# K and Q turned in one transfer, k turned in its own order, later loads on the Pool queue, a shorter mask product and a plan tuned anew, in a kernel of a long convolution and a memory attention

## Chip, cores and metric

One core of one Trainium2 chip. The time is device microseconds of one execution. A profile is one execution with the hardware profiler on; its span is from the first to the last instruction, some 2 us shorter than the time of the same execution. "Granted clock" is the share of its full rate that TensorE was granted, averaged over the span.

## The reference, cut to what matters

Two independent parts stand side by side; their outputs are concatenated. All data are bf16.

```python
# part A: S = 2048 positions, 640 channels
k_shift = sum(k_pad[:, t:t + S] * shift_k[:, 3 - t] for t in range(4))   # 4 taps
kv = k_shift * v
y = causal_convolution(kv, ssm_k) + kv * ssm_D       # by Fourier transforms in the reference
a = q * y

# part B: x is 2048 x 640, 32 heads of 20, N = 4 segments of L = 512
for s in range(4):
    logits = qs @ ks.T * scale + mask                # causal inside a segment
    o = g * (phi(qs) @ M) / (phi(qs) @ z) + (1 - g) * softmax(logits) @ vs
    M, z = M + phi(ks).T @ vs, z + phi(ks).sum()
b = concat_heads(o) @ wo
```

## The kernel before

Python records every operation with a key, prices it, and a list scheduler (`plan`) fixes one order for each engine from priorities; `BIAS` and `HOLD` are tables of tuned corrections to them. So an edit of a table or a price can move any instruction. The queue of an engine is in order, its DMA issues included.

Part B runs in 8 units (4 segments times 2 halves of the heads). A unit projects x to K, Q and V, turns K and Q (so that the head dimension lies on the partitions), bounds the logits from the largest |K|, and makes scores, exponential and products.

```python
def wload(engs, half):            # weights; w0: first half of the heads, w1: second half
    def f():
        for i, (w, eng) in enumerate(zip((B_wk, B_wq, B_wv), engs)):
            eng.dma_start(out=self.wqkv[:, :, half, i, :], in_=...)
# "w0", "w1", "wo", "Wf", "Wi" and xT all load from nc.sync (SP)

def proj(tci):                    # four token blocks a unit; KQ has two buffers
    KQ = self.KQ[:, tci % 2]
    for i in range(3):
        ...                       # five products of xT and wqkv
        nc.scalar.copy(out=dst, in_=...)                 # the cast to KQ or Va
    nc.sync.dma_start_transpose(out=self.KTs[u][:, :, tok], in_=KQ[:, 0, :, :])
    nc.sync.dma_start_transpose(out=QT[:, :, tok], in_=KQ[:, 1, :, :])

def bound():
    V.tensor_reduce(out=kam[:], in_=self.KTs[u][:], axis=AX.X, op=ALU.max, ...)   # needs only K
    ...                           # A = sel * kam; PqT = phi(QT)
    V.tensor_scalar(out=qabs..., in0=QT..., ...)         # |Q|, needs Q
    for g in range(4):
        nc.tensor.matmul(pb[0:16, :], lhsT=A[:, g, :], rhs=qabs[:, g, :], ...)    # "tq,A" in the profile

def attn(g):
    ...
    if masked:
        for hl in range(4):
            nc.tensor.matmul(st[:, hl, 0:384], lhsT=self.ident[:], rhs=self.nmask[:], start=True, stop=False)
    for (kc, c0) in spec:         # scores on top of it, four row strips at once
        ...
# [cut: part A loads v and q in four pieces each from nc.sync, and turns k in four strided transfers to kr]
```

The softmax here doesn't subtract the row's maximum and nothing guards it: scores larger than these inputs give would overflow.

## Time and profile before

| | before |
|---|---|
| time, median of 3 | 328.97 us (328.57 to 334.71) |
| span of the profile | 331.0 us, granted clock 0.975 |
| TensorE / VectorE / ScalarE busy | 287.2 / 272.7 / 266.0 us |
| first product | 12.56 us |

The prediction shows the lines of the page and of the timeline. In a timeline line the columns are start, duration, engine and source line, operation, output and inputs, shapes, count, and in brackets the engine's idle time before it and what ended that. All operations carry the line of one helper, so tiles are told apart by name.

One thing the prediction did not read belongs here too. Before the change the work of the bound falls in two steps, the largest of K (`kam`) while Q's turn is still on its way:

```profile
25.18 2.29 DVE L441 TENSOR_REDUCE kam<-KT 128x4 f32<-128x2048 bf16 x1 [0.82 <-DMA KT<-KQ]
27.50 0.23 DVE L441 TENSOR_TENSOR A<-sel,kam 128x64 bf16<-128x64 bf16 x1
29.60 0.69 DVE L441 TENSOR_SCALAR tq<-QT 128x2048 int16<-128x2048 int16 x1 [1.87 <-DMA QT<-KQ]
```

(VectorE's timeline, kernel before, first unit.) VectorE waits for K 0.82 us and for Q 1.87 us; the 2.29 us in between cost nothing. TensorE, in the same unit, waits for the last of these three:

```profile
30.35 1.35 PE L441 MATMUL ab<-tq,A 128*16 128x512 bf16 x4 [1.52 <-DVE tq L441]
```

### The profile page before, as it was taken

The numbers are of one execution on the slowest core, as the hardware profiler recorded it, in microseconds if no ns is written. First come the engines' busy times: TensorE is split into PE (matmuls) and PEld (weight loads), VectorE is DVE, ScalarE is ACT, GpSimd is POOL, SyncE is SP. The second block draws the span as 40 slices with busy tenths as digits, with TensorE's granted clock in tenths as the row PEclk, the third lists the DMA queues.
The fourth block names the chain that finished last, engine by engine and source line by source line (L and its number), as shares of the span: only waits on it lengthen the run. The fifth ranks groups of instructions, "written<-read, shape, count | busy, mean of one in ns | idle before, by whom it ended". The sixth has DMA issues, their size and how long they took to land. (4 is left out here: it accounts for less than half of the span.)

```text
span 331.0 us, 8829 instructions
## 1 busy us (share of the span) xinstructions
PE 287.2 (87%) x3673; PEld 199.6 (60%) x3674; DVE 272.7 (82%) x455; ACT 266.0 (80%) x351; POOL 30.4 (9%) x58
## 2 busy tenths in 40 slices
PE   0498899989999995999999995999989997897982
PEld 0375766666767674566857662676765664564641
DVE  0016859999998979999997597799999999999942
ACT  1176699799998998899898887878899999668711
POOL 5001100000000010000101010300010001330310
PEclk9998999999999999799999998999999999998998
DMA  8945954646405986813321669504303452324272
GB/s 251 224 95 125 253 95 94 124 125 111 81 2 141 201 136 155 209 50 81 70 59 53 119 135 188 139 6 77 66 20 69 60 79 60 98 49 126 66 138 79
DMA packets 97159, 35.65 MB, mean 108 GB/s; under 512 B 90000, under 2 KB 95168, under 8 KB 96864
## 3 DMA queue, kind: packets, MB, share of 16 engines
q1 hardware_dynamic: 94816, 30.01, 43.7%
q0 software_dynamic: 1872, 4.76, 5.5%
q8 instruction: 28, 0.46, 0.6%
q10 hardware_dynamic: 432, 0.34, 0.3%
q14 instruction: 11, 0.09, 0.1%
HBM read 13.46 MB, written 5.24 MB: 56 GB/s over the span
## 5 line engine op out<-in xcount | busy, mean ns | idle before, releaser
L441 ACT ACTIVATE ET<-st 128x1536 bf16<-128x1536 f32 (+1 forms) x96 | 154.9, 1614 | 23.1 <-PE st L441 22.4
L441 PE MATMUL ab<-wqkv,xT 128*128 128x320 bf16 x480 | 75.9, 304 | 13.3 <-DMA wqkv<-in_B_wk_dram 12.6
L441 PEld LDWEIGHTS <-xT 128*128 128x128 bf16 x480 | 45.1, 99 | 33.3 <-DMA xT<-in_B_x_dram 10.6
L441 PEld LDWEIGHTS <-ET 128*128 128x128 bf16 x1280 | 42.3, 96 | 10.2 <-issue 6.6
L441 ACT CAST F<-ab 128x512 bf16<-128x512 f32 x80 | 45.4, 615 | 2.3 <-PE ab L441 1.6
L441 PE MATMUL o<-Va,ET 128*128 128x21 bf16 x1280 | 44.1, 173 | 2.3 <-DVE o L441 1.9
L441 PE MATMUL st<-QT,KT 32*128 32x128 bf16 (+3 forms) x512 | 34.8, 303 | 8.7 <-ACT ET L441 8.5
L441 ACT CAST KQ<-ab 128x320 bf16<-128x320 f32 x64 | 28.0, 461 | 14.9 <-PE ab L441 14.4
L441 DVE TENSOR_TENSOR S<-S 128x2048 bf16<-128x2048 bf16 (+1 forms) x40 | 37.0, 941 | 0.0
L441 PEld LDWEIGHTS <-Wf 128*128 128x128 bf16 x320 | 28.1, 97 | 11.8 <-issue 7.9
L441 PE MATMUL st<-nmask,ident 128*128 128x384 bf16 x128 | 26.4, 329 | 2.8 <-ACT ET L441 2.7
L441 PEld LDWEIGHTS <-KT 32*128 32x128 bf16 x512 | 11.8, 91 | 28.2 <-issue 26.3
L441 PE MATMUL ab<-wo,oT 128*128 128x320 bf16 (+1 forms) x140 | 22.4, 300 | 4.1 <-ACT outb L441 3.5
L441 PE MATMUL ab<-kT,Wf 128*128 128x256 bf16 x160 | 23.6, 273 | 0.9 <-ACT F L441 0.2
L441 POOL DMA_DIRECT2D out_dram<-outa x20 | 15.3, 767 | 93.0 <-DVE outa L441 85.3
L441 DVE TENSOR_TENSOR o<-o,rr 128x320 bf16<-128x320 f32 x48 | 23.2, 484 | 0.5
L441 PE MATMUL ab<-vt,Wf 128*128 128x256 bf16 x160 | 22.0, 273 | 1.3 <-DVE vt L441 1.2
L441 DVE TENSOR_TENSOR ET<-ET,cmask 128x1024 bf16<-128x1024 bf16 x32 | 21.6, 675 | 1.6 <-ACT ET L441 1.6
L441 DVE TENSOR_TENSOR S<-Xh,Kh 128x4096 bf16<-128x4096 bf16 x10 | 22.8, 2278 | 0.0
L441 PEld LDWEIGHTS <-oT 128*128 128x128 bf16 x160 | 14.1, 100 | 13.7 <-issue 6.5
L441 PE MATMUL ab<-skd,kr 128*128 128x128 bf16 x320 | 22.0, 227 | 0.3 <-DVE vt L441 0.2
L441 DVE RECIPROCAL rr<-o 128x16 f32<-128x16 f32 (+1 forms) x64 | 15.3, 239 | 7.3 <-PE o L441 7.3
(70 smaller groups left out, 402.7 us busy)
## 6 DMA issues: line engine op xcount, KB each, us to landing
sk<-in_A_ssm_k_dram SPq DMA_DIRECT2D x5, 512.0 KB, 3.9
vt<-in_A_v_dram SPq DMA_DIRECT2D x20, 128.0 KB, 3.2
qd<-in_A_q_dram SPq DMA_DIRECT2D x20, 128.0 KB, 3.3
out_dram<-outa POOLq DMA_DIRECT2D x20, 128.0 KB, 2.6
out_dram<-outb POOLq DMA_DIRECT2D x12, 160.0 KB, 2.6
Wf<-c_wf SPq DMA_DIRECT2D x1, 1024.0 KB
Wi<-c_wi SPq DMA_DIRECT2D x1, 1024.0 KB
wqkv<-in_B_wq_dram SPq DMA_DIRECT2D x2, 400.0 KB, 5.5
```

Of the source, the lines that this page charges most:

```text
L441: f(*[fix(a) for a in args], **{k: fix(v) for k, v in kw.items()})
```

## The change

The intent: fewer issues on the SP queue, which is late with its turns, and less TensorE time.

```diff
-    nc.tensor.matmul(st[:, hl, 0:384], lhsT=self.ident[:], rhs=self.nmask[:], ...)
-    for (kc, c0) in spec:
+    nc.tensor.matmul(st[:, hl, 0:256], lhsT=self.ident[:], rhs=self.nmask[:], ...)
+    parts = ... if not masked else [(3, 0, 0, 128), (2, 128, 0, 128), (2, 128, 128, 256)]
+    for (kc, c0, a, b) in parts:          # the last part has no mask under it and starts its own sum

-    nc.sync.dma_start_transpose(out=self.KTs[u][:, :, tok], in_=KQ[:, 0, :, :])
-    nc.sync.dma_start_transpose(out=QT[:, :, tok], in_=KQ[:, 1, :, :])
+    nc.sync.dma_start_transpose(out=self.KQT[half][:, :, :, tok]..., in_=KQ...)

-    kr = ring("kr", [128, 4, KPAD + 512]); for c in range(4): dma_start_transpose(kr[:, c, ...], k rows c::4)
+    kr = ring("kr", [128, KPAD + S]);      for n in range(2): dma_start_transpose(kr[:, 1024 n ...], k rows in order)
-    lhsT=kr[:, cc, p0:p0 + 128]
+    lhsT=kr[:, first:first + 509:4]

-    "Wi": nc.sync ...   "w1": (nc.sync,) * 3   "wo": nc.sync ...   vt, qd: nc.sync
+    "Wi": nc.gpsimd ... "w1": (nc.gpsimd,) * 3 "wo": nc.gpsimd ... vt (but the first), qd: nc.gpsimd
# [cut: prices of two kinds of operation, how BIAS and HOLD enter plan, finer keys, and both tables anew]
```

The last cut is no detail: with it every engine gets another order. On SP the first loads, `Wf, sk, x, wq, wk, ident, wv` before, become `wk, wq, Wf, x, wv, sk`.

## The prediction

> **What bounds the kernel now.** I read the page first (busy shares, slices), then the waits, then the timeline of single stretches where TensorE stood still, and then single tiles.
>
> ```profile
> PE 287.2 (87%) x3673; PEld 199.6 (60%) x3674; DVE 272.7 (82%) x455; ACT 266.0 (80%) x351; POOL 30.4 (9%) x58
> ...
> PE   0498899989999995999999995999989997897982
> ```
>
> TensorE is the fullest engine, and in the second line (40 slices of 8.3 us, tenths) it stands at 9 or more nearly everywhere between the first two slices and the last two; slices 16 and 25 are the deep dips. VectorE and ScalarE follow at 80%, so there is no single owner: TensorE bounds the middle when nothing blocks it, and a chain of matmul, exponential, matmul (one PSUM area "st" for all scores) takes over where it is blocked. I split TensorE's 331.0 - 287.2 = 43.8 us of idle time: 12.6 us before the first product, about 7.5 us after 318.2 us (the drain: 12.8 us with some 5 us of products in it), so about 23.7 us in the middle. The middle is thus 93% full. Its largest holes, from the timeline of TensorE and of ScalarE:
>
> ```profile
> 12.56 2.83 PE L441 MATMUL ab<-wqkv,xT 128*128 128x320 bf16 x10 [12.56 <-DMA wqkv<-in_B_wk_dram]
> ...
> 128.40 1.91 ACT L441 ACTIVATE PqT<-QT 128x2048 bf16<-128x2048 bf16 x1 [1.05 <-DMA QT<-KQ]
> ...
> 131.70 0.40 PE L441 MATMUL st<-QT,KT 32*128 32x512 bf16 x4 [2.52 <-ACT ET L441]
> ```
>
> ```profile
> 201.03 1.91 ACT L441 ACTIVATE PqT<-QT 128x2048 bf16<-128x2048 bf16 x1 [2.89 <-DMA QT<-KQ]
> ...
> 203.31 0.84 PE L441 MATMUL ab<-wo,oT 128*128 128x320 bf16 x5 [3.23 <-ACT outb L441]
> ```
>
> Both dips have one story: ScalarE, in order, stands before the exponential of the turned Q, which waits for its transfer; then that 1.91 us exponential goes ahead of the work that would free PSUM, and TensorE stops for 2.52 and 3.23 us. Why the transfer is late shows in the timeline of the SP queue just before the second:
>
> ```profile
> 190.16 1.90 SPq L441 DMA_DIRECT2D qd<-in_A_q_dram  x3
> 192.16 1.25 SPq L441 DMA_TRANSPOSE QT<-KQ  x1
> 193.45 0.59 SPq L441 DMA_DIRECT2D qd<-in_A_q_dram  x1
> 194.14 2.13 SPq L441 DMA_TRANSPOSE KT<-KQ  x1
> 196.38 1.20 SPq L441 DMA_TRANSPOSE QT<-KQ  x1
> 197.68 4.24 SPq L441 DMA_TRANSPOSE oT<-o_s  x3
> ```
>
> The queue issues without a break: a load of q for a later stage (2.5 us in four pieces) stands between the turns of K and Q, and the last turn of Q begins to be issued only at 196.38.
>
> **What the Trainium skill says.** (1) "Perfetto Trace Analysis", section "What 'DMA-bound' means", says that a queue solid with issue slices shows descriptor generation rather than data movement; the section "DMA Optimizations" advises spreading issues over the engines that can issue. The SP queue above agrees. (2) "DMA: Bandwidth & Descriptors", "SWDGE vs HWDGE vs iDMA": issues from Pool have their descriptors written by software on Pool's cores, and a plain DMA transpose must come from SP or ACT; so only the plain loads can move, as done. (3) "SBUF — State Buffer", "SBUF: two separate sides": VectorE operations in a two-port mode lock Pool out while it writes descriptors. In this trace Pool's 20 stores of 512 pieces took 750 to 907 ns with VectorE 82% busy, so I see no starvation. (4) The same page, "Door 1: The DMA port swizzle", says that a stride is free while consecutive accesses share a 16-byte line, for bf16 up to 8 elements. The trace has such a case, below, and agrees.
>
> **The change part by part.**
>
> *Mask product.* The timeline of one masked block:
>
> ```profile
> 40.88 0.81 PE L441 MATMUL st<-nmask,ident 128*128 128x384 bf16 x4 [0.54 <-ACT ET L441]
> 41.62 0.34 PE L441 MATMUL st<-QT,KT 32*128 32x128 bf16 x8
> ```
>
> One such matmul takes 326 ns (median), four overlap into 0.81 us, so they follow at (0.81 - 0.326) / 3 = 161 ns, which is 384 columns at 2.4 per ns (estimate from these rows). At 256 columns that is 107 ns: 4 x 54 = 0.216 us less for each of 32 blocks, 6.9 us. Against it the 256-wide score product of each head is cut into two 128-wide ones, 128 more matmuls and weight loads (3674 to 3802). Short matmuls follow at about 25 ns (28 of "o" in 0.85 us), so 4 x 25 = 0.1 us a block as the most, 3.2 us; about half if the shorter streams overlap as four row strips do. Net: 3.7 to 5.3 us of TensorE time, taken as 4.5. It lies in the middle, which is 93% full, and also in the chain through "st": I count 4 of it.
>
> *K and Q in one transfer, k in its own order.* 64 issues of 1.22 us become 32 of double size, 20 issues of k at 1.26 us become 10. The issue of xT, five times the size, took 2.78 to 3.35 us, so one more 128 KB costs 0.4 to 0.5 us; a double one some 1.7 us (estimate). SP time: 78 + 25 = 103 us become 54 + 17 = 71 us. The bytes stay. K's turn now waits for Q's cast too (about 0.5 to 1 us later for the bound), while Q lands about 0.6 us sooner.
>
> *Weights of k with a stride of 4 elements.* The load of sk has this stride today: its weight loads take 113 ns in the median, those of kr 98. But the rate counts:
>
> ```profile
> 36.02 1.07 PE L441 MATMUL ab<-skd,kr 128*128 128x128 bf16 x16
> 36.92 0.61 PE L441 MATMUL ab<-ident,sk 128*128 128x128 bf16 x8
> ```
>
> A single one lasts 219 ns in both, so the spacing is (1.07 - 0.22) / 15 = 57 ns without and (0.61 - 0.22) / 7 = 56 ns with the stride. I count zero; the weight-load rows alone will grow by 320 x 15 ns = 4.8 us, hidden.
>
> *Plain loads to Pool.* 16 vt, 20 qd, three weights, Wi and wo leave SP: 36 x 0.6 + about 2.5 = 24 us of SP queue. With the turns SP is relieved of some 56 us, a sixth of the span. Pool's busy time rises from 30.4 to about 60 us (36 x 0.76 + 5 x 0.6), which costs nothing by itself. What the two queue parts gain are the stalls behind late turns: 2.52 + 3.23 us, and 0.76 + 0.51 + 1.04 us at the neighbouring waits of the same pattern (also at 240 us), 8 us in all. Half is kept back, since the exponential of the turned Q still occupies ScalarE: 4 us.
>
> *Start and drain.* The new order brings wk and wq ahead of Wf and xT, and sk behind. The first product needs wk and xT: 0.4 + 0.4 + 1.0 + 0.64 MB stand at or ahead of xT, where 2.95 MB stood ahead of its last need before. But 0.4 to 1.2 MB of weights of the second half now start on Pool at once and share the 16 DMA engines. I take 1 us. At the end eight products of part A move behind the first twelve of the last projection, where TensorE waited for the last turn: 0.5 us.
>
> *New priorities.* All orders change. The rest of the middle's holes, some 16 us, may grow or shrink; I take zero, with 4 us to each side.
>
> Sum: 4 + 4 + 1 + 0.5 = 9.5 us off 329.0, so **319.5 us**.
>
> **The rivals.** (a) *The chain through "st" holds:* each head group makes three rounds of scores and exponential (1.90 and twice 1.47 us of ScalarE, 155 us in all), and with ScalarE at 80% and VectorE at 82% the freed TensorE time turns into waiting for "ET". For it: 12.4 us of TensorE's waits are on ET today. Against: nearly all of those holes are short, and the long ones come from the late turn. It would give 324 to 327. (b) *Pool's queue becomes the in-order trap that SP was:* loads of v and q now stand behind stores that wait for their results (85 us of such waits by Pool). If they come late, the products of v stall. Against: v and q are issued a stage ahead, and landing took 2.6 us from Pool and 3.2 us from SP. It would give 325 to 332. (c) *The new order is better than its parts:* with 282 us of TensorE work, a middle filled to 95% rather than 93% ends near 11.5 + 279 / 0.955 + 12.8 = 316; with less waiting at the start, 313.
>
> **Range and chances.** My number is the sum of the parts; (c) sets the low end, 313.5, (a) the high end, 326. Faster by 2% means under 322.4, inside the range and 3 us above my number, so faster 0.67, same 0.31. Slower would need (b) in full: 0.02.
>
> **What would show it right or wrong.** Right: TensorE busy near 282 to 283 us; the mask product at about 272 ns a piece and 0.54 us for four; spacing of the k products still 57 ns while their weight loads take 113 ns; 42 turns fewer on SP, SP's breaks back; no wait over 1 us of ScalarE for the turned Q; the holes of 2.5 and 3.2 us gone. Wrong in the mask step: the twelve short score products last over 0.45 us. Wrong in the queue step: VectorE or TensorE wait for vt or qd, or TensorE's idle time in the middle stays near 24 us with other releasers. Wrong in the start: a first product later than 12.6 us, because the Pool loads take the DMA engines.

## The result and the profile after

The changed kernel takes 345.5 us (median of 4, 344.28 to 348.43), against 330.39 us (median of 4) of the kernel before: ratio 1.049, interval 1.038 to 1.060, so slower by 5%, where 3% faster was predicted. All four of its runs are fast; of the four of the kernel before, one (334.71 us) counts as slow and is left out of the ratio. The granted clock of the two profiles is the same (0.976 and 0.975). A ratio here is the mean time of one kernel's fast runs over the mean of the other's fast runs of the same rounds, so not quite the ratio of the quoted medians. Runs over 1.5% above the fastest of their kernel count as slow. The kernel before scatters by some 3% (328 to 338 us), so the mean of its fast runs depends on its fastest run; where a verdict is fine I give the medians too (they are over all runs, slow ones included).

The page after:

```profile
PE 283.5 (83%) x3801; PEld 199.4 (58%) x3802; DVE 272.6 (80%) x455; ACT 265.4 (78%) x351; POOL 61.6 (18%) x99
...
PE   0058799799898799998779979999979998788892
```

TensorE is busy 3.7 us less, Pool twice as long, both much as predicted. The slices (8.5 us each here) show where time went: two empty ones lead, not one, and the third is half full (before it stood at 9).

```profile
20.89 8.31 PE L442 MATMUL ab<-wqkv,xT 128*128 128x320 bf16 x45 [20.89 <-DMA xT<-in_B_x_dram]
```

(TensorE's timeline, after.) The first product starts at 20.89 us instead of 12.56, and waits for x's turn instead of wk. From first product to end it is 321.0 us, before 318.4: so 8.3 of the 10.9 us of longer span lie ahead of the first product, and the other 2.6 us, where 4 us and more of gain were expected, lie behind. The start on SP and on Pool (timelines, after):

```profile
0.74 0.46 SPq L442 DMA_DIRECT2D wqkv<-in_B_wk_dram  x1
1.25 0.51 SPq L442 DMA_DIRECT2D wqkv<-in_B_wq_dram  x1
1.81 0.52 SPq L442 DMA_DIRECT2D Wf<-c_wf  x1
2.38 8.46 SPq L442 DMA_TRANSPOSE xT<-in_B_x_dram  x1
```

```profile
3.89 0.86 POOL L442 DMA_DIRECT2D wqkv<-in_B_wv_dram  x1
...
7.40 0.88 POOL L442 DMA_DIRECT2D wqkv<-in_B_wk_dram  x1
```

1.8 MB (wk, wq, Wf) are issued ahead of x's turn, and while it is under way (from 2.38 us to its landing at 20.89) Pool starts two 0.4 MB loads of second-half weights (and at 12.87 us a third), which nothing needs yet. Before, x's turn was issued at 1.64 us, behind Wf and sk.

```profile
8.00:18.00 10.00, 0.00 (x0) 0.00 (x0) 0.00 (x0) 0.00 (x0) 1.15 (x2) 1.00 1.25 135
```

(Stretches, after; the last two columns are the DMA share and GB/s.) From 8 to 18 us the DMA engines are full, with packets overlapping (1.25), but move only 135 GB/s. Before, from 8 to 14 us, they moved 279 GB/s:

```profile
8.00:14.00 6.00, 1.44 (x6) 0.94 (x7) 0.00 (x0) 0.00 (x0) 0.00 (x0) 1.00 1.15 279
```

Why the rate is so low isn't settled: b_w1_pool below, with the same loads from Pool beside x's turn, moved 290 GB/s in the same stretch.

The second place is a pause at 113 us. Timelines after of ScalarE, TensorE, SP and Pool, in this order:

```profile
112.97 0.42 ACT L442 CAST KQ<-ab 128x320 bf16<-128x320 f32 x1 [3.53 <-DMA KQT<-KQ]
```

```profile
113.45 1.19 PE L442 MATMUL ab<-wqkv,xT 128*128 128x320 bf16 x5 [3.55 <-ACT KQ L442]
```

```profile
105.36 4.90 SPq L442 DMA_TRANSPOSE KQT<-KQ  x2
```

```profile
101.47 2.96 POOL L442 DMA_DIRECT2D vt<-in_A_v_dram  x4 [22.29 <-PE ab L442]
104.42 0.55 POOL L442 DMA_DIRECT2D Wi<-c_wi  x1
```

The cast may not write its buffer of KQ until the joint turn has read it; that turn, issued at 105.36 us, lands 7.5 us later (3.4 us in the median), with the 1 MB of Wi and four pieces of v in flight. The two pauses that the prediction aimed at are gone from their places, but this one stands in, and another of their kind appears where no turn is late:

```profile
256.67 0.34 PE L442 MATMUL st<-KQT 32*128 32x384 bf16 x4 [2.66 <-ACT ET L442]
```

Ahead of it ScalarE starts the exponential of the turned Q at 252.89 us without any wait; its 1.96 us stand before the exponential that TensorE needs.

The prediction's details held: mask products of 273 ns, four in 0.60 us (0.54 was predicted, but its own figures, 0.81 less 0.216, make 0.59); the twelve short scores 0.34 us; sixteen products of kr in 1.06 us, so still 56 to 57 ns apart.

```profile
49.39 0.60 PE L442 MATMUL st<-nmask,ident 128*128 128x256 bf16 x4 [0.16 <-ACT ET L442]
49.92 0.34 PE L442 MATMUL st<-KQT 32*128 32x128 bf16 x12
```

### The profile page after: what moved, and what is told of

Same layout as the page of the kernel before. It is cut to its first block, busy times and chain, and to the rows that moved or that the text cites. A ratio compares the mean times of both kernels' runs of the same rounds, so it can differ in the third digit from the quotient of the medians.

```text
span 341.9 us, 8967 instructions
## 1 busy us (share of the span) xinstructions
PE 283.5 (83%) x3801; PEld 199.4 (58%) x3802; DVE 272.6 (80%) x455; ACT 265.4 (78%) x351; POOL 61.6 (18%) x99
## 4 chain that ended last, share of the span: by engine, by line
PE 36%; ACT 20%; DVE 19%; DMA 12%; issue 9%; POOL 1%; SPq 1%; ACTq 0%; DVEq 0%; POOLq 0%
PE ab L442 25%; ACT ET L442 10%; PE st L442 6%; DMA xT<-in_B_x_dram 5%; PE o L442 5%; DMA KQT<-KQ 5%; DVE Xh L442 4%; DVE S L442 4%; ACT F L442 4%; ACT KQ L442 2%; DVE ET L442 2%; DMA out_dram<-outb 2%; DVE o L442 1%; DVE kam L442 1%; ACT kT L442 1%
## 5 line engine op out<-in xcount | busy, mean ns | idle before, releaser
L442 PE MATMUL ab<-wqkv,xT 128*128 128x320 bf16 x480 | 77.5, 309 | 25.4 <-DMA xT<-in_B_x_dram 20.9
L442 PEld LDWEIGHTS <-xT 128*128 128x128 bf16 x480 | 45.3, 100 | 47.2 <-DMA xT<-in_B_x_dram 20.9
L442 ACT CAST KQ<-ab 128x320 bf16<-128x320 f32 x64 | 26.5, 436 | 32.9 <-PE ab L442 28.5
L442 PEld LDWEIGHTS <-ET 128*128 128x128 bf16 x1280 | 41.6, 96 | 17.5 <-issue 12.6
L442 ACT CAST F<-ab 128x512 bf16<-128x512 f32 x80 | 44.4, 627 | 2.4 <-PE ab L442 2.0
L442 PE MATMUL st<-KQT 32*128 32x128 bf16 (+2 forms) x640 | 35.0, 275 | 6.1 <-ACT ET L442 5.7
L442 DVE TENSOR_SCALAR xm<-KQ 128x640 bf16<-128x640 bf16 x12 | 3.8, 318 | 30.6 <-ACT KQ L442 30.6
L442 PEld LDWEIGHTS <-KQT 32*128 32x128 bf16 x640 | 13.3, 92 | 23.6 <-issue 21.4
L442 PE MATMUL ab<-kT,Wf 128*128 128x256 bf16 x160 | 22.6, 273 | 2.5 <-ACT kT L442 1.1
L442 PE MATMUL st<-nmask,ident 128*128 128x256 bf16 x128 | 19.3, 273 | 4.4 <-ACT ET L442 3.8
L442 POOL DMA_DIRECT2D vt<-in_A_v_dram x16 | 11.9, 752 | 54.4 <-PE ab L442 34.7
```

What stands on the lines that cost most here:

```text
L442: f(*[fix(a) for a in args], **{k: fix(v) for k, v in kw.items()})
```

## The experiments

**Theories.** S (start): x's turn shares the DMA engines with weights loaded ahead of it and beside it from Pool, and the late first product moves the whole kernel. J (joint landing): one transfer of K and Q takes from the bound the step in which K was worked on while Q travelled. N: the new order is the worse one, rather than (P) bulk loads on Pool in the middle that delay turns. M: the loss lies in the middle, not at the start. Rivals in each case: the time would stay when the part is undone.

Fourteen kernels ran (a gap in the table: the profile fell on a slow execution). In each, the engines' order was kept and only the named operations were changed after planning. All gave right results. The kernel before had medians of 333.1, 333.1, 332.8, 332.8 and 332.9 us in the five sessions, of which the first three ran on one chip and the other two on two others. The medians in the table are over all runs (a_split's and b_rest's take in one of 862 and one of 629 us), the ratios over the fast ones.

| run | base | what differs | median us | ratio (95%) | first product us | clock |
|---|---|---|---|---|---|---|
| after | | the change | 345.5 | 1.049 (1.038–1.060) | 20.89 | 0.976 |
| a_w1_sp | after | w1 on SP, behind sk | 337.3 | 1.015 (1.012–1.019) | 14.01 | 0.973 |
| a_split | a_w1_sp | K and Q turned singly | 336.1 | 1.018 (1.011–1.025) | | |
| a_order | a_split | and v, q, Wi, wo on SP | 335.7 | 1.013 (1.007–1.018) | 13.40 | 0.979 |
| a_xfirst | after | x first on SP | 334.1 | 1.011 (1.007–1.015) | 7.53 | 0.970 |
| a_both | a_xfirst | and w1 on SP | 334.9 | 1.015 (1.010–1.021) | 7.57 | 0.970 |
| a_xsplit | a_xfirst | K and Q turned singly | 332.9 | 1.003 (1.000–1.005) | 7.71 | 0.981 |
| b_w1_pool | before | w1 early on Pool | 335.7 | 1.008 (1.004–1.012) | 16.72 | 0.985 |
| b_mask | before | mask product only | 329.3 | 0.990 (0.986–0.994) | 12.37 | 0.982 |
| b_turns | before | joint turn, k in own order | 349.7 | 1.052 (1.048–1.056) | 12.39 | 0.970 |
| b_kq | before | joint turn only | 350.0 | 1.059 (1.049–1.068) | 12.41 | 0.957 |
| b_kr | before | k in own order only | 332.0 | 1.005 (1.001–1.008) | 12.41 | 0.992 |
| b_pool | before | v and q on Pool only | 333.2 | 1.006 (1.002–1.010) | 12.34 | 0.977 |
| b_rest | before | mask, k, v and q | 331.6 | 0.996 (0.993–0.999) | 12.58 | 0.977 |
| b_start | b_mask | x first on SP | 327.2 | 0.985 (0.978–0.992) | 7.93 | 0.990 |

### The start

**a_w1_sp.**

```diff
+ w1 = [o for o in order if o.key[:2] == ("load", "w1")]    # second-half weights
+ each of w1: issued by sync instead of gpsimd, right behind sk
```

> The changed kernel with its orders kept on every engine, except that the three weight loads of the second half (wqkv, 400 KB each) are issued from SP right behind sk instead of from Pool at once. Theory S (sharing): in the changed kernel these loads, started on Pool at 3.9 and 7.4 us, take turns with the first turn of x on the 16 DMA engines and make it land at 20.9 us. Then the first product comes at 12 to 14 us here and the whole is 7 to 9 us shorter than the changed kernel (345.5 down to about 337.5, still 2% above the kernel before). Rival O (order on SP): wk, wq and Wf ahead of xT are what makes it late; then the first product stays near 20 us and the time does not move by more than 2 us.

8.2 us faster than the changed kernel (medians), first product at 14.01 us.

```profile
14.01 8.63 PE L442 MATMUL ab<-wqkv,xT 128*128 128x320 bf16 x45 [14.01 <-DMA xT<-in_B_x_dram]
```

So loads that nothing needed, only started early from another queue, held x's turn back by 6.9 us, and the end followed: by 8.2 us in the medians, of two sessions, by 4.5 us in the spans of the two profiles (341.9 to 337.4). The rest to 12.56 us, 1.5 us, I put down to the order on SP itself (wk and wq ahead of x's turn). The Trainium skill, "DMA: Bandwidth & Descriptors", section "Issuing engines are not separate DMA queues", says that transfers of all issuing engines run on the same 16 DMA engines and interleave. This run agrees, and puts a price on it.

**b_w1_pool**, the same loads moved the other way in the kernel before:

```diff
+ each of w1: issued by gpsimd instead of sync, near the start of Pool's queue
```

> The kernel before with its orders kept, except that the same three loads go to Pool, right after its first constant, at about 3.9 us. The reverse test. S: xT lands late and the first product moves from 12.6 us to 17 to 21 us, the time grows by 4 to 8 us (to 333 to 338). O: the first product stays within 1.5 us of 12.6 and the time within 2 us.

The first product moved by 4.2 us, 12.56 to 16.72, so sharing holds in this order too: x's turn landed 11.8 us after its issue instead of 8.9. Both figures fall a little short of theory S's (17 us and 4 us): the median moved only by 2.6 us. A late start is not always paid one to one.

**a_xfirst**, only the order of six loads of the changed kernel:

```diff
- sync: wk, wq, Wf, x, wv, sk
+ sync: x, wk, wq, wv, Wf, sk
```

> The changed kernel with only the first six loads on SP in another order: x first, then wk, wq, wv, Wf, sk (it had wk, wq, Wf, x, wv, sk). The three second-half weights stay early on Pool. Theory S (the loss is at the start, because x's turn shares the DMA engines and comes last): x's turn is then issued before Pool's first bulk load starts at 3.9 us; first product at 8 to 12 us instead of 20.9, and the time falls by 7 to 12 us: ratio 1.013 to 1.028. Theory M (the new order loses it in the middle): the first product comes earlier, but the end moves by less than 4 us: ratio over 1.037.

```profile
0.74 2.79 SPq L442 DMA_TRANSPOSE xT<-in_B_x_dram  x1
```

```profile
7.53 1.49 PE L442 MATMUL ab<-wqkv,xT 128*128 128x320 bf16 x5 [7.53 <-DMA wqkv<-in_B_wk_dram]
```

(SP and TensorE of a_xfirst.) The early Pool loads are all still there. Ahead of them, x's turn is issued in 2.79 us instead of 8.46, and the first product comes at 7.53 us. The time falls by 11.4 us (9.6 by the spans), within the 7 to 12 us expected. Theory S holds, and by the medians no other single edit of the changed kernel gains as much; but the first product is now 5 us ahead of the kernel before, so this is more than the start had lost.

**a_both** moves the second-half weights back as well.

> The same order of first loads, and the second-half weights also on SP behind sk. The version with those weights on SP alone had 1.0153 with its first product at 14.0 us. Theory S: first product at 8 to 9 us, and the end follows by 4 to 6 us: ratio 0.997 to 1.004. Theory M: 1.010 or more.

A miss. The first product is as early as in a_xfirst, and the span equal (332.4 and 332.3 us), so once x is first, the Pool loads at the start cost nothing visible. The expected 0.997 to 1.004 did not come: the ratio is 1.015, which is theory M's, by medians 1.006 (334.88 over 332.79). The session had a fast run of the kernel before (328.27 us), which lowers the mean of its fast runs. By ratio the end did not follow the earlier first product at all (a_w1_sp has the same 1.015), by span it followed by 5.0 us (337.4 to 332.4), by medians by 2.4; which of these is right the runs don't settle. What is safe is that a first product 5 us ahead of that of the kernel before doesn't make this kernel faster than it: something else costs.

### The joint turn

**b_turns** puts the joint turn and k's own order into the kernel before:

```diff
- sync.dma_start_transpose(K half); sync.dma_start_transpose(Q half)
+ sync.dma_start_transpose(K and Q)        # where the later of the two stood
- four strided turns of k; + two in its own order
```

> The kernel before, same order of every engine, with K and Q turned in one transfer (at the place of the later of the two) and k turned in two transfers in its own order and read with a stride. My prediction's step: about 3 to 4 us less, because the waits of ScalarE for the turned Q (1.05, 2.89, 0.92 us) shrink. Rival W: the merged transfer lands later than the first of the two did and keeps both halves of KQ from being rewritten until then; then casts into KQ wait, the gain is under 1 us or it is slower. The strided weights should cost nothing: spacing of the k products 57 ns with weight loads of 113 ns.

16.6 us slower than before (medians): as much as the whole change. Rival W has the direction right and its sign is there (casts into KQ wait 4.0 us for the joint turn), but 4.0 us is not 16.6. **b_kq** and **b_kr** part the two:

```diff
b_kq:  + the joint turn of K and Q alone
b_kr:  + k in its own order alone
```

> The kernel before, same order of every engine, with only K and Q turned in one transfer (k as before, in four). Theory J (joint landing): what cost 17 us in the run with both turns merged is that the reduction of K (2.29 us on VectorE, eight times) now waits until Q has landed too, while it used to run during Q's turn. Then this run is again about 15 to 17 us slower than before (near 348), VectorE waits for the merged transfer before the reduction by 12 us or more in sum. Rival R (k's order or its strided weights): this run is within 3 us of the kernel before.

> The kernel before, same order, with only k turned in its own order, two transfers in place of four, read with a stride of 4. J: within 1.5 us of the kernel before, spacing of the k products unchanged at 57 ns. R: slower by 10 us or more.

b_kr is neutral, so the stride of the weights of k is free, as counted, and halving its issues gains nothing. b_kq alone is 16.9 us slower. Waits of VectorE for `kam`, before and in b_kq (columns: us in all, times, longest):

```profile
DVE kam L441 <- DMA KT<-KQ: 1.0, 2, 0.8
```

```profile
DVE kam L441 <- DMA KQT<-KQ: 17.8, 8, 6.3
```

In all eight units VectorE, in order, now stands before the reduction. First unit of b_kq, VectorE and TensorE:

```profile
31.68 2.29 DVE L441 TENSOR_REDUCE kam<-KQT 128x4 f32<-128x2048 bf16 x1 [6.27 <-DMA KQT<-KQ]
34.00 0.23 DVE L441 TENSOR_TENSOR A<-sel,kam 128x64 bf16<-128x64 bf16 x1
34.14 0.68 DVE L441 TENSOR_SCALAR tq<-KQT 128x2048 int16<-128x2048 int16 x1
```

```profile
34.88 1.87 PE L441 MATMUL ab<-tq,A 128*16 128x512 bf16 x4 [5.00 <-DVE tq L441]
```

The reduction starts at 31.68 instead of 25.18 us: the last half to land now releases both. The 2.29 us of K's work, once beside Q's turn, lies on the path, and TensorE's pause grows from 1.52 to 5.00 us. Of the 4.5 us by which TensorE's product comes later (34.88 against 30.35), K's work is thus 2.3; the other 2.2 go with the later landing of Q's half. Nor did the queue get its time back: three joint turns in a row take

```profile
20.14 7.72 SPq L441 DMA_TRANSPOSE KQT<-KQ  x3
```

2.57 us each, while a free joint turn is issued in 1.27 us, a single one in 1.22. Theory J's time and waits came in the old order; how much of the 16.9 us is K's lost step and how much the later landing, no run separates. One caution: keeping the old order is harsh on the joint turn, since the reduction stays placed for an early K.

**a_split** turns K and Q singly in the changed kernel's order (on top of a_w1_sp):

```diff
- sync.dma_start_transpose(K and Q)
+ sync.dma_start_transpose(K half); sync.dma_start_transpose(Q half)
```

> The changed kernel with the weights of the second half on SP (as in the run a_w1_sp) and, new, K and Q turned in two transfers again, K first, at the place of the merged one; all else and all orders kept. J: the new order already sets the reduction of K late (it waits 1.2 us in all), so the joint landing costs little here: 0 to 3 us less than a_w1_sp. If the merged transfer still holds the chain here, 4 us or more less.

No difference from a_w1_sp beyond the intervals: in the changed kernel's order VectorE waits only 1.2 us in all for the joint turn ahead of the reduction, against 17.8 us in b_kq, so the new order had placed it late already. One execution of this kernel, the profiled one, took 862 us, and its profile isn't used. **a_xsplit** repeats the split on top of a_xfirst:

> The version with x first, with K and Q turned in two transfers, K first. If the joint turn makes the 3.45 us pause at 103 us: the pause waiting for KQ goes (K's half of the buffer is free earlier), with it one of the five half-clock stretches (1.71 us each), together 3 to 5 us: ratio 0.996 to 1.003. If the bulk load of Wi on Pool makes it (it shares the DMA engines with either form of turn): the pause stays over 2 us and the ratio is 1.007 to 1.014.

1.0025 against 1.0111: a gain of 0.9% by the ratios, 0.4% by the medians (334.1 to 332.9), while the pause stays:

```profile
101.29 0.84 PE L442 MATMUL ab<-wqkv,xT 128*128 128x320 bf16 x5 [2.81 <-ACT KQ L442]
```

So each expectation got one half right: the time is the first one's, the pause (2.81 us after 3.45) the second one's. Wi was issued 0.6 us ahead of the turns in this run too. In a_order, with Wi on SP behind the turns, this pause is gone; TensorE waits 1.30 us for Wi itself instead. I take the pause as made mainly by the bulk load beside the turn, and the joint turn as costing 0 to 3 us in the new order (a_split shows no gain, a_xsplit 1 to 3 us).

### The remaining parts

**b_mask:**

```diff
- matmul(st[:, hl, 0:384], ident, nmask);  + matmul(st[:, hl, 0:256], ident, nmask[:, 0:256]) and three score parts
```

> The kernel before, same order of every engine, with the mask product 256 wide and the third score product cut in two (the mask constant stays 384 wide in memory). My prediction's step: 4 us less (about 325 against 329), one mask product 272 ns, TensorE busy near 282.7 us. Rival (chain through st holds): TensorE's busy time falls the same, the time by 0 to 1.5 us only, and idle time before score products grows by what was saved.

3.9 us faster by medians, 3.3 by the ratio of 0.990. This is the part of the change that pays.

**b_pool:**

```diff
- v (from the second chunk on) and q: sync;  + gpsimd
```

> The kernel before, same order, with the 16 later loads of v and the 20 loads of q issued from Pool. My prediction's step: the stalls behind late turns of Q shrink (2.89 and 1.05 us of ScalarE), 2 to 4 us less. Rival (in-order trap or sharing): loads wait behind stores, or turns land later because Pool's loads take turns with them; then 0 to 4 us more.

No gain; 1.006 is on the rival's side. Some 22 us less on SP's queue (36 issues of 0.6 us) did nothing for the time, although in this profile the stalls that the prediction counted on did shrink: ScalarE waits 1.2 us for the turned Q, once, instead of 4.9 us. Such waits vary between profiles (3.8 us in b_mask, 4.7 us in b_rest, which has the same loads on Pool), but nothing of them came through to the time here: those stalls were not worth what they measured.

**b_rest**, mask product, k's own order and Pool loads together in the old order:

> The kernel before, old order, with the shorter mask product, k in its own order and vt and qd on Pool: all parts of the change that were neutral or good alone. If the parts add, 0.990 x 1.0045 x 1.006 = 1.001, so 0.996 to 1.006; if k's shorter queue time and the Pool loads help only once SP and TensorE are both relieved (they work together), under 0.988.

0.996: the parts simply add, within their intervals; no part helps another. (One of its 22 runs took 629 us and is left out; its profiled run counts as slow.)

**a_order**, the changed kernel with the Pool loads, the joint turn and the early weights undone:

```diff
  (a_split)
- vt, qd, Wi, wo: gpsimd
+ vt, qd, Wi, wo: sync, at the places of the new order
```

> The changed kernel with three parts undone: the second-half weights on SP right behind sk, K and Q turned separately (K first), and vt, qd, Wi and wo on SP, at the places where the new order has them. What stays is the new order of every engine, the shorter mask product and k in its own order. With the old order those two give 0.990 x 1.0045 = 0.995 of before. Theory N (the new order itself costs the rest): ratio 1.012 to 1.022, like the version with the Pool loads (1.018). Theory P (the bulk loads on Pool delay the turns, the 3.4 us hole at 106 us): ratio 0.993 to 1.003, and the hole that waits for KQ disappears. First product near 14.0 us under both.

1.0126. Its two remaining parts would make 0.995 in the old order, so the new order costs some 1.8% (6 us), of which about 1 us is the first product at 13.40 us. One rival stays: the loads put back on SP stand where the plan had placed them for Pool's queue. The profile shows little of that (ScalarE waits 2.0 us for the turned Q, TensorE 1.3 us for Wi and for no load of v or q), but no run separates it from the order. This is Theory N's number, although one of Theory P's signs, the pause before KQ gone, is there too.

**b_start**, the best version: the old order, the mask product, and x first:

```diff
- sync: Wf, sk, x, wq, wk, ident, wv, skc
+ sync: x, wk, wq, wv, ident, sk, Wf, skc
```

> The kernel before with the shorter mask product and the first loads on SP put in another order: x first, then wk, wq, wv, ident, sk, Wf, skc (before: Wf, sk, x, wq, wk, ident, wv, skc). 1.5 MB no longer stand ahead of what the first product needs: first product at 8.5 to 10 us instead of 12.4. If the start shifts the whole kernel: ratio 0.979 to 0.984. If the work behind it waits for sk, Wf or k instead, as the early move of the three weights showed (first product 4.2 us later, end 2.6 us later): 0.985 to 0.992.

```profile
7.93 2.83 PE L443 MATMUL ab<-wqkv,xT 128*128 128x320 bf16 x10 [7.93 <-DMA wqkv<-in_B_wk_dram]
```

327.2 us, ratio 0.985 (0.978 to 0.992), two of the six runs being slow. It is at the better end of the second expectation, and that one's sign is there: TensorE waits 1.3 us for sk and 0.6 us for k. The version is faster than both kernels, though not surely by 2%.

### Where the clock comes in

In the profiles looked at closely TensorE's granted clock is full but for stretches of 3.4 us at half, or two or three of them in a row. In the changed kernel each of the four in the middle begins within 2.2 us of the end of a pause of 1.16 to 3.55 us; in other profiles a few stand without one (at 304 us in the kernel before). The pause of 3.55 us at 113 us above, before the stretch and during it (stretches, after: columns are the window, its length, TensorE busy, weight loads, VectorE, ScalarE, Pool, granted clock, DMA share, GB/s):

```profile
111.50:113.50 2.00, 0.05 (x1) 0.05 (x1) 1.09 (x2) 0.53 (x2) 0.00 (x0) 1.00 0.59 127
113.75:117.25 3.50, 3.50 (x42) 2.18 (x41) 1.83 (x5) 3.50 (x5) 0.00 (x0) 0.51 0.39 78
```

42 matmuls in 3.50 us at half clock, 27 in the 2.00 us from 117.50 us, at full clock. So such a pause is paid twice: by its length, and by 1.71 us (the missing half of the stretch) afterwards. The Trainium skill, "TensorE: Matmul & The Clock Gate", section "Part 1: The HAM clock gate", tells of such a gate, with half rate until some 3.4 us of work; the length agrees. Busy time thus isn't work: a_xfirst has five such stretches between 40 and 320 us and TensorE busy 286.5 us, b_start one, and 279.4 us, for the same count of matmuls but one. It doesn't separate the two kernels of this case (four stretches each, granted clock 0.975 and 0.976), but it does separate versions: one minus the granted clock, times the span, is 3.2 us in b_start, 5.9 in b_mask, 10.0 in a_xfirst and 15.0 in b_kq.

## Why the prediction was wrong, by its own steps

- **Mask product: right.** "I count 4 of it": 3.3 to 3.9 us measured alone.
- **Two slips in its reading.** After 318.2 us TensorE has 5.9 us of products, not 5, so the middle has 24.4 us without work and is 92% full, not 93. And the last turn of Q, issued at 196.38 us, was used only at 201.03: 4.65 us, where 2.5 us is the median landing. So the queue explains only part of that stall.
- **Start: wrong in sign and size.** The step is "But 0.4 to 1.2 MB of weights of the second half now start on Pool at once and share the 16 DMA engines. I take 1 us." It saw the load that shares, and counted bytes ahead of the last need. What counted is what was in flight beside x's turn (135 GB/s moved where it was 279 before): the first product came 8.3 us later instead of earlier, 6.9 us of it by the Pool loads alone. Moving these back gives 8.2 us; putting x first, which goes beyond undoing it, 11.4 us. The prediction had named the sign that would show it wrong, "a first product later than 12.6 us, because the Pool loads take the DMA engines", but gave it no weight in the range.
- **The queue parts: wrong.** "What the two queue parts gain are the stalls behind late turns", 8 us, half kept. The stalls did go: ScalarE's waits for the turned Q fell from 4.9 to 1.0 us. The gain didn't: v and q on Pool alone make 1.006 (with those waits at 1.2 us), k alone 1.005, and in the changed kernel casts of KQ wait 4.1 us for the joint turn, with a 3.55 us pause of TensorE behind them. The stall moved from the reader of the turn to the writer of its source. And the pause of 2.66 us at 254 us shows that the exponential's place alone makes such a pause, with no turn late.
- **Joint turn.** The step "K's turn now waits for Q's cast too (about 0.5 to 1 us later for the bound), while Q lands about 0.6 us sooner" missed that the bound used the time between the two landings. The joint turn alone, in the old order, costs 16.9 us, and the new order hides most of it, leaving 0 to 3 us. Its estimate of 1.7 us for a double issue was off both ways: 1.24 us in the median after, 2.57 in a row on a busy queue.
- **Weights with a stride: right.** Still 56 to 57 ns apart; b_kr neutral. The weight load itself isn't free: 114 ns in the median after, 98 before, hidden.
- **New priorities: zero was wrong.** a_order puts them at about 6 us of loss (with the reservation made there), beyond the 4 us to each side.
- **Drain:** not tested by itself.

The miss is 24.6 us (9.5 faster predicted, 15.1 slower in that session's medians). Start 9 to 12 (8.2 to 11.4 lost and the 1 us not gained), queue and joint turn 4 to 7 and the order about 6 come near its size, but they come from different sessions and overlap by about 1 us in the first product, so the sum is no proof. Of the rivals, (a) is not what happened (waits on ET 12.4 us before, 12.1 after); (b) pointed at Pool's queue, but for another reason: no product waited long for v or q; bulk transfers slowed SP's turns.

What stays open: what in the new order costs its 6 us. In the profiles a_order has 3.4 us more TensorE time left than b_mask at 40 us and 2.8 us more at 300 us, which speaks for the first 40 us; but these profiles differ by less than the runs scatter, and a_both, with an early start, did not come out clearly better.

## What to carry to other kernels

Ahead of the first product ask of every transfer in flight, on any queue, whether something needs it sooner than the one that the first product waits for; put that one first, and let bulk loads of later stages start behind it. Before merging two transfers, look at what the readers do between the two landings and when the writers get their buffers back. A plan made anew is a change of its own: measure it with the parts undone, and measure each part in the old plan.

## What the Trainium skill lacked or had wrong

- "DMA: Bandwidth & Descriptors", section "Issuing engines are not separate DMA queues": right that all queues share the engines, but without a size. Here unneeded loads from Pool moved the landing of a turn issued on SP from 14.0 to 20.9 us, and with the turn issued first they cost nothing visible (a_xfirst and a_both).
- The same page gives no time to landing of turns between on-chip tiles (it has a bandwidth of DMA transposes, and sequencer cycles). Here a turn of 128x512 landed 2.5 us after its issue (median) and one of 128x1024 3.4 us, 7.5 us beside a bulk load; issue took 1.22 and 1.24 us, and 2.57 in a row.
- "TensorE: Matmul & The Clock Gate", section "Part 1: The HAM clock gate": gives an idle window of some 3.4 us as what brings half rate; of short idles it says that they can do so too, without a length. Here half-rate stretches of 3.4 us also followed pauses of 1.2 to 3.6 us (not all of them: 1.57 us at 27 us in b_start had none), and the loss over the span reached 10.0 of 332 us in a_xfirst and 15.0 of 349 in b_kq.
- No page tells of single executions that take 1.9 to 2.6 times as long (629 us in b_rest, 862 us in a_split), each once in a kernel whose other runs agree within about 2%.
